# A fused set-attention and gated feed-forward kernel: centring with two-tensor instructions, GpSimd's issues ahead of its weight cast, and another written order of steps

## The chip, the cores and the metric

The kernel runs on one core of a Trainium2 chip. The core has a matrix engine (TensorE, PE in the profile, with its weight loader PEld), three engines for elementwise work (VectorE = DVE, ScalarE = ACT, GpSimd = POOL) and a queue engine (SyncE = SP). Each engine works through its own queue in order; they wait for each other by semaphores. Transfers are issued from the queues of SyncE, ScalarE or GpSimd and carried by 16 shared DMA engines. The metric is the device time of one execution, in microseconds.

## The reference

Four batches `b` of N = 12416 rows of x, each row with C = 128 numbers, meet m = 32 inducing rows.

```
def mab(q, kv):
    s = scale * (q @ kv.transpose(0, 2, 1))
    s = s - s.max(-1, keepdims=True)
    a = np.exp(s)
    a /= a.sum(-1, keepdims=True) + 1e-09
    return a @ kv
h = mab(I, x)           # [B, 32, 128]: one pass over all rows of the batch
y = mab(x, h)           # [B, N, 128]
gate = np.maximum(y @ w_gate, 0.0)      # 128 -> 1536
val = y @ w_val
out = gate * val @ w_out                # 1536 -> 128
```

All inputs and the output are float32.

## The kernel before, in words

Each output row depends on x only through its 32 attention weights over `h`. Where the sign of each gate is the same for all rows of a batch, the output is a quadratic form of these weights; the kernel works out its tables once for each batch, so that the feed-forward layer over 1536 hidden units is done on the 32 rows of `h` and not on 12416 rows of x. Checks of this run along, and a slow general kernel stands behind a branch at the end; it doesn't run here.

**Rows and tiles.** A batch is cut into six blocks `q` of 16 tiles of 128 rows (`CT = 16`, `NQ = 6`) and a remainder of one tile. `Q` counts these blocks over all batches, 0 to 23, and 24 is the four remainders together.

**The head** (`first_batch`, L264 to L450) reads batch 0 in float32 parts on SyncE's queue, casts them (L370), turns them on TensorE (L380), weighs and sums them for `h` of batch 0. The order of that is the text `HEAD`. At its end stand the weights: GpSimd casts `w_gate` to `wg` (L441), then issues the load of `w_out` to `wo` (L442) and the seven loads of batch 1 (`load_x`, L237: six of 16 tiles and the remainder, cast to float16 on the way); ScalarE casts `w_val` to `wv` (L443). Then comes `centre(0, ...)`.

**centre** (L244 to L262) makes `h` from its sums (L247, a `scalar_tensor_tensor` with two tensors), and writes it into `hT` in three copies: centred by its mean (L250), and plain twice (L254); L262 adds the mean. All are small: 128 partitions by 32 or 16 numbers. TensorE's gate matmuls (L890) need `hT`, and behind them come the tables of the batch.

**The rest** is a list of some 1,600 steps, each with its engine or engines, what it needs and which buffers it takes. What sets the order of the work on every engine is the text `ORDER`: each word of it names a step by its place in the list, the engine by a digit, and the buffers that it takes (`Plan.run`). The steps that the prediction speaks of, by the names in the code:

- `load` (GpSimd, L237): issue the load of a block; `turn` (SyncE, L763, a transposing transfer) or `tp` and `tc` (TensorE L774, then a copy L779 or L781): turn the block. `s1`, `p1`, `hz`, `ha`: weigh the block and add to the sums of `h` of its batch.
- `hw` (VectorE, L829): `zs` = the stacked identity times the weights' sums; `join` (TensorE, L839): add them over partitions; `centre` (VectorE).
- `gate`, `on`, `v`, `u`, `uj`, `tm`, `tab`, `lin`, `L`: the tables of a batch (products on VectorE or GpSimd at L980, table matmuls L999, scaling to the table `T` on ScalarE at L1011 or VectorE at L1013).
- `s2`, `p`: scores of a block and their exp (ScalarE, L514). `d`: differences of the weights (L561), two PSUM banks at once (`dd`) and two more in `mb`. `f2`: squares of two banks (ScalarE, L575). `fc`: the two single banks, squared on ScalarE (L587) or only copied on VectorE (L589); after a copy comes `fm`, a multiplication by itself (L593) on GpSimd or VectorE. `pp`, `zq`: squares (L524, L544) on either.
- `o`, `ol`: output matmuls (L619, L608); `e`: division (VectorE, L649); `st`: store (SyncE).
- `keep_busy` (L1168): filler matmuls ahead of some `d` steps.

GpSimd and VectorE steps whose kind stands in the list `shared` (L1175) are tied by hand: each GpSimd step of such a kind waits for the last VectorE step of such a kind that stands ahead of it in `ORDER` (`in_turn`, L1178). `centre` and `load` are not on that list; `hw` is.

Of the kernel before, what the change touches and what calls it, by code (L numbers as in the profile page):

```python
# [12 lines left out]
ALU = mybir.AluOpType  # L13
# [90 lines left out]
LK4LL464s4Mp4Ly4364Lz496c4LU0Ov00Le0MG000050Oz04Lo0Oy2Ow2Ox2P02O+2011O-2P1030U0M60P3012e0220600050P  # L104
21P412f10u0310710v10A10IB014B0J1PH2PE2PI2PD20CC023APb0Pc050810M10D10E1PP0PQ00Pd00304PR0PS0Pe0Pf00K1
0G1Pg1PF2PC2042PB2PG20O00429LW0810Q10P10S1053P63LX2LY03EU0PT0PJ0PK05PL00+00418LZ2PU10-1PV2PM0122PN0
Lg073PW02P53PO1101P721G00017PX0Li05Ls0040w300232Pa2Lh2Lj2Lt21K11H11I1Ck0P8011A002360x05PA11B10d000f
00g00Z041M00y2P921E21C10W014005151m0300e01621510h20M+01e020b01d00a07U0Me0Ni0Lq05H+01n1182Lr22E01y00
0341z10Y01+11330z31F31o310c22021i011j01c01P01s005431b01u11w11t11g0M8030MA03La005GE01h00o041f25M92Lb
12800202MB21k20X03MI050l00m00j00p01l4OD4NK4N940i4291MJ12A12C21922g2222001012422622310q0LQ0150r0Lc02  # L110
0k0LR10s240n22q001001732D3MR32u12r11X05A60LS04Lk0031Y0MS31213LT22s2Ld2Ph24O001Ll11O042w0012BMT04P1L
m031V02x12y2Ln2Lu0101W02+21Z21Lv14U001394Y14V11T02Q02M20001S0Lw052O04W2M31Md304Q30Mo322t3Mz332k0031
A2l12m11R01Q02N01p002P0Lx22o21q21r31U24X33W05030001072G033X1M4044R052I02R224S2311321M522722p2253MC0
123c005462K0MK0012J02L0MD13g1ML12M23e13413d1ME02MM042T012h05Mi013Mg00MF2MN2MO22i2Mj2MP022U03o00455N
V0Mh1N834NJ352z3NU32j32H03MQ22V02W02Y03Z002a03p13s13q1Pm022X233a2Pp2Pn2Po22b02Z0Pq01Pr13u000583v12c
2Pi04Ps023+03M013L03C033B03A03Y313b34T32-3Pt1Pj2Pl2Pk23i00423Pv2Pu23w13y1P-23k13j13m1Pw23O0FM03G003
I03S053703D03N0P+33P253E203T03F03R04m004213Q04q14o14n13U25k42S4Is41a4NL42Ok4O24Mq453V42d4N20413H04I
03Bs04E02700525G040N323J2Px015H1711Py1Pz1Q12Q624104a000424L0NX054D04J0MX0714c14e14b1Q02Q700Q804K04G
0NY24g00454QB1Q22QC24k14i14h143004504204F04407305QD04QE0Q334M22MY2742QH14H240035S0015749046215U25C0
45D0Mk0124705A05T1Ml15W1Q52Q424A05e000104804B25g15i15f1MV024-055205109E0MW25B050057004w01QI2NA464C4  # L120
5Y0032A4t05Z15a15c1QO353255E234z04y04x0550A+0580MZ0055604+259268041Ma15M0031BQJ026915O2QK06B05Dc05J
005443K45F4OO44N45N1QN26C25K26A32QP04QQ05P25Q16E00325Mb055+00N0016G2QT26F16I16K00346Ng35I31Nh315L37
230Mc2N126O26L15z0Mm056005-05q026M1Mn25V26W001485l0535t05p05w05u05v06a16X161216Y28m0405x256Q000138n
16R1650Mv0055o05r06406U26S2Mw16H36P38o316T3Ns305s2N40147C00104N517E27G26V37D17u051Mx026306207v1NF00
47I00109662My2NG1N6057J1NH03674OZ48M4Nt4N727M1NQ012O132OC33ON346Z36D37O004517Q17K1NI27S2Nk083Nm00Nl
27P1NR16r046y057x016s06z06t06m036x0Nn27y27H2QU276000126d027826w06h06i06u06l0NZ0007717A1Na16+207T37w
327936v26o08A005108B18C26n06p23NS00Nb049e052Ke06g08E1NT27+0030A9f1Nc26j0753Nd27F38D36k2Ne017k047m07
# [12 lines left out]
1B-02C00Cd3DA32CP3Cg2Cf1Ot03Bx01E305C10E42Ou2Bu0Ci1DQ00450C20DU1Bw0CC00Bz0By0C324DR1B+2CB0RM05DS1DE  # L140
0032ABN4AV4RN2RP2DF1CA0CD0Ch3DD3CX3Bv01RO2DI2DG1DJ3E231CE25DK00458DL1DO2E53DP3RS02C80C70RI03RQ00DM1
RT2RL2RJ2E600524E71RR2EA2RK2C60Eu041C50Cq00Co0Ev1E81C92Rg2Ra2DW00237Cm04Cu0Cr0Ct0Cw0Cp0DX1DY1Da1Cv0
F400151D002Cz0Fm030F51Cs23Re2Cx2Rb2Fn1D300C+0D40C-0Cn0Fy00349F61F81Fz1Ew30D121D50D20Dl01Do0Dm0EO005
23D62G01F+1Rd2Rc2Ri2CF4Cy4C446-4D74ES1Dj00Dw04Dg0Dh0Dx0Dy0Dn0EP1De0EQ1EI00322EK1Dp25RV3RU3EB3Dz0Ro0
Di0EJ1Dk2Rj05Dr03Rk0Df0Rn2EM1EC00105D+23ED1EG2Du0Dt0Eb05Ds0Ge022Rh2EE1E+0040BGf1Ea0Rp01EZ0F02E-1Ex0
2EH3Rq0Rr0Ey2F21Gk00426Rs0Dv2Rf2Gl1Ee00Ef0Ed0Eg0Rt2Ru2EW0FA0031AGo1Gm1EY0El02Eq04Ek0Er0FB1Eh24Ec2RW
2FC1FE1EX0Fs00057Ep0Em0Eo0Ft1R+3Fu2Es20RX03Fw1FG00100RY2RZ1FH1FI2FK2Rv04Rw0Ej0IO051Rz1G200318En2IP1
FR00R-04FS0Fp02FJ2G31G62Fq2D-4Et4BC4Dq4S00FL3Ez3S32RH2Fo22F13Fr3FO05G41Ia00122Ib1FV0FQ0FT0FU21FX0FW
0FY0G800435Ic1Ie1FZ2G91Fj00Fi0Fb01HW020FP0IQ31GA2GC2GB2HX1Gq00543Gu2Gr1Fc0Fh0Fd0Fg0GO03GD3Gv3G73Fk2
3Gs1Gw00244Fe0GN0GP0GL05Gx1G+2GG0Gy1Hu00041Ff2GK0GJ0GZ01GY0GQ0GI0Hv1G-3Hy2Fv3Gg30Hw1Hc0024AGR20Gb0H  # L150
d1IR00GW03GU0GV0Hg2GH0IS2GM2He1H00040BH42H11GT0Ga0HH05HG0HB02Gc22H53HY32H80H21GX2Ho00010Hq2Hp1HF0Gh
04GS4Fa4Fl4Gi2Gj3Hz3HC0HI0HD0L4032Hs2IU00045HA0HJ25L51Ht3Hr3HN01HL0HO0IV1HE2IY2H903IW1Hi00529Hj1Hk2
HM0HZ00HR0HS0KA040HT0Ha2HP20Hm1Im00507HQ0KB1In1IF01IE0IL02I10Io1Iq2KM00408Hb3Hl3Hh3HU2KN1KQ2ID0L703
II0IG0L82SA2IK0IJ0KO1KY00503KZ1IM21Kc2IH2I403I804I70I30I00Ka1Ig00204Ih1Ik2I90IA0I50I20IB23Ir3IT3KC3
0JG011Ii1KG0050BJH1KH1KI1I62Iy04I-02J10Iw0Ix0Iz0J703J50KK2HV4HK4Gd4Jk4KS00106IZ2S92S72KL2It05I+20J0
0J20KU1KT1KW1J32J60J80JA0JD0K-01J925Je00429Il3JI32Ji2Jf1JC0Kk00KD03K+0Kj0JB0KE2JE2Jj3KF3Jg1JM00230K
# [11 lines left out]
def square_body(ctx, tc, x, inducing, moe_w_gate, moe_w_val, moe_w_out, out):  # L168
    nc = tc.nc
    B, N, C = x.shape  # L170
    M = inducing.shape[0]
    DFF = moe_w_gate.shape[1]
    P = 128
# [70 lines left out]
    def centre(b, sums):  # L244
# [8 lines left out]
        for o, n in ((M, M), (2 * M, H)):  # L253
            nc.vector.tensor_scalar(  # L254
                out=hT[b][:, o : o + n],
                in0=h[:, 0:n],
# [7 lines left out]
    def first_batch(sp, psum):  # L264
# [179 lines left out]
        for q in range(NQ + 1):  # L444
            load_x(1, q, x16q[q] if q < NQ else x16r[1])
# [952 lines left out]
```

## Time and profile before

| | us |
|---|---|
| median of 3 runs | 240.14 |
| lowest and highest | 238.80, 240.24 |
| the profiled execution | 240.26 |
| its span, first to last instruction | 238.4 |
| granted TensorE clock, share of full | 0.994 |

The busy times of the page are sums over the span: TensorE 222.7, VectorE 205.4, ScalarE 201.7, GpSimd 128.7 us. A busy TensorE is not TensorE at its peak, since matmuls overlap and their ends are modelled. In a row of the timeline the columns are start and duration in us, engine, line, operation, written tile <- read tiles, and in brackets the engine's idle time ahead of it with what ended that. Lines are those of the kernel before.

### The profile page before, as it was taken

What the parts mean: (1) busy time and instruction counts of PE and PEld (TensorE: products, weight loads), DVE (VectorE), ACT (ScalarE), POOL (GpSimd) and SP (SyncE); (2) the same over time, 40 slices, a digit from 0 to 9 for tenths busy, and PEclk for the clock granted to TensorE, in tenths of its full rate; (3) what the DMA queues carried; (4) which work ended last, traced back from release to release, by engine and by line L of the source; (5) the groups of instructions that cost most, each with busy time, mean ns of one, the idle gap of its engine ahead of it and who ended that gap; (6) DMA issues with size and microseconds to landing.
All of it is one profiled execution on the core that took longest, in us unless ns stands there. A gap on an engine that the chain in (4) does not pass through costs nothing.

```text
span 238.4 us, 9612 instructions
## 1 busy us (share of the span) xinstructions
PE 222.7 (93%) x4092; PEld 174.3 (73%) x4092; DVE 205.4 (86%) x433; ACT 201.7 (85%) x366; POOL 128.7 (54%) x164
## 2 busy tenths in 40 slices
PE   5869888999999999999999999998999999999990
PEld 1768457787787888887788778875787777777870
DVE  4665798899589999869999999899999998989792
ACT  3665798799999889898989988898999999998940
POOL 4444905619493139795731527687143568963900
PEclk9999999999999999999999999999999999999997
DMA  6998899989998698969995999121292060665764
GB/s 212 413 396 317 99 214 204 197 160 191 197 202 219 150 272 308 245 109 236 289 269 99 265 168 411 50 116 64 91 355 88 4 267 3 268 247 206 287 228 151
DMA packets 36240, 49.25 MB, mean 207 GB/s; under 512 B 24384, under 2 KB 25056, under 8 KB 36192
## 3 DMA queue, kind: packets, MB, share of 16 engines
q1 hardware_dynamic: 31568, 38.64, 50.5%
q0 software_dynamic: 4576, 9.93, 23.7%
q8 instruction: 33, 0.54, 0.9%
q14 instruction: 15, 0.12, 0.2%
q10 hardware_dynamic: 48, 0.02, 0.1%
HBM read 27.80 MB, written 25.43 MB: 223 GB/s over the span
## 4 chain that ended last, share of the span: by engine, by line
PE 66%; DMA 16%; DVE 11%; ACT 3%; issue 2%; POOL 0%; SPq 0%; DVEq 0%; ACTq 0%
PE mb L619 34%; PE dd L561 7%; DMA x<-in_x_dram 6%; DMA x16q<-in_x_dram 6%; PE mb L561 4%; PE mb L608 4%; DVE osb L649 4%; DMA w<-in_moe_w_val_dram 4%; PE mb L804 3%; PE mb L505 3%; PE mb L790 3%; PE mb L774 2%; PE mb L999 2%; ACT F L575 2%; DVE F L589 2%
## 5 line engine op out<-in xcount | busy, mean ns | idle before, releaser
L619 PE MATMUL mb<-T,F 128*128 128x128 f16 x1536 | 107.8, 219 | 0.1
L575 ACT ACTIVATE F<-dd 128x1024 f16<-128x1024 f32 x97 | 100.1, 1032 | 9.2 <-PE dd L561 4.0
L619 PEld LDWEIGHTS <-F 128*128 128x128 f16 x1536 | 87.4, 98 | 18.1 <-issue 16.6
L593 POOL TENSOR_TENSOR F<-F 128x512 f16<-128x512 f16 x59 | 60.6, 1042 | 31.8 <-DVE pp L524 8.8
L587 ACT ACTIVATE F<-mb 128x512 f16<-128x512 f32 x120 | 69.1, 607 | 2.9 <-PE mb L561 1.6
L649 DVE TENSOR_TENSOR osb<-mb,zr 128x512 f32<-128x512 f32 x97 | 64.4, 680 | 6.2 <-PE mb L619 4.2
L589 DVE CAST F<-mb 128x512 f16<-128x512 f32 x74 | 49.6, 683 | 4.2 <-PE dd L561 2.6
L561 PE MATMUL mb<-p,diff 32*128 32x512 f16 (+1 forms) x200 | 39.8, 376 | 0.0
L561 PE MATMUL dd<-p,diff 32*128 32x512 f16 (+1 forms) x200 | 37.6, 375 | 1.4 <-ACT F L575 1.3
L524 POOL TENSOR_TENSOR pp<-p 128x512 f16<-128x512 f16 (+1 forms) x21 | 21.2, 1010 | 12.4 <-PE mb L619 5.5
L561 PEld LDWEIGHTS <-diff 32*128 32x128 f16 x400 | 13.8, 91 | 10.8 <-issue 5.2
L999 PE MATMUL mb<-wo,U 128*128 128x128 f16 x264 | 18.7, 219 | 0.0
L994 POOL TENSOR_TENSOR U<-U,U 128x1536 f16<-128x1536 f16 x3 | 9.3, 3099 | 16.7 <-DVE zr L544 7.8
L999 PEld LDWEIGHTS <-U 128*128 128x128 f16 x264 | 15.2, 97 | 1.8 <-issue 1.6
L514 ACT ACTIVATE p<-mb 128x512 f16<-128x512 f32 (+1 forms) x25 | 14.7, 593 | 2.0 <-PE mb L505 1.1
L608 PE MATMUL mb<-L,pp 32*128 32x128 f16 x384 | 16.2, 216 | 0.0
L980 DVE TENSOR_TENSOR U<-ga,va 128x1536 f16<-128x1536 f16 x15 | 14.4, 969 | 0.2
L980 DVE TENSOR_TENSOR U<-va,ga 128x1536 f16<-128x1536 f16 x15 | 14.5, 970 | 0.0
L384 DVE COPY xT<-xT_ps 128x1024 f16<-128x1024 f16 (+1 forms) x15 | 8.6, 581 | 5.9 <-PE xT_ps L380 5.9
L370 POOL CAST x16f<-x 128x512 f16<-128x512 f32 (+2 forms) x14 | 7.4, 531 | 11.4 <-DMA x<-in_x_dram 11.4
L370 ACT CAST x16f<-x 128x512 f16<-128x512 f32 (+2 forms) x15 | 7.8, 517 | 6.8 <-DMA x<-in_x_dram 6.7
L608 PEld LDWEIGHTS <-pp 32*128 32x128 f16 x384 | 10.1, 93 | 4.6 <-issue 0.5
(158 smaller groups left out, 305.2 us busy)
## 6 DMA issues: line engine op xcount, KB each, us to landing
out_dram<-osb SPq DMA_DIRECT2D x44, 512.0 KB, 4.4
x16q<-in_x_dram POOLq DMA_DIRECT2D x18, 512.0 KB, 9.4
x<-in_x_dram SPq DMA_DIRECT2D x9, 512.0 KB, 7.1
out_dram<-osb SPq DMA_DIRECT2D x9, 256.0 KB, 2.0
x<-in_x_dram SPq DMA_DIRECT2D x6, 256.0 KB, 9.2
w<-in_moe_w_gate_dram SPq DMA_DIRECT2D x1, 768.0 KB, 8.3
w<-in_moe_w_val_dram SPq DMA_DIRECT2D x1, 768.0 KB, 8.9
wo<-in_moe_w_out_dram POOLq DMA_DIRECT2D x1, 384.0 KB, 5.6
```

The source lines that it names most:

```text
L370: f(out=dst[:, a:b, :], in_=x32[:, a:b, :])
L524: engines[e].tensor_tensor(out=p2b[slot["pp", Q]][:, 0:w], in0=a, in1=a, op=ALU.mult)
L561: nc.tensor.matmul(bs[r][:, o], diff[rows, 4 * jj : 4 * jj + 4, :].rearrange("p k m -> p (k m)"), pb[slot["p", Q]][rows, 0:w], start=True, ...
L575: act.activation(out=Fb[slot["F", Q, j]][:, pair(j), :], in_=dd, func=AF.Square, accum_out=None if k is None else spread(Q, k),)
L587: act.activation(out=dst, in_=src, func=AF.Square, **more)
L589: dve.tensor_copy(out=dst, in_=src)
L593: engines[e].tensor_tensor(out=a, in0=a, in1=a, op=ALU.mult)
L608: nc.tensor.matmul(mb[slot["m", "o", Q, r]][:, t * P : (t + 1) * P], p2b[slot["pp", Q]][rows, t * P : (t + 1) * P], L[(Q // NQ) % 2][rows, :],
L619: nc.tensor.matmul(ps[:, t * P : (t + 1) * P], Fb[slot["F", Q, j]][:, r, t * P : (t + 1) * P], T[Q // NQ][:, j, :], start=start, stop=stop,)
L649: dve.tensor_tensor(out=o[:, 4 * (r % 2) : 4 * (r % 2) + 4, :], in0=mb[slot["m", "o", Q, r]].rearrange("p (t c) -> p t c", t=4), in1=rz.un ...
L980: engines[e].tensor_tensor(out=U[i][:, :, 4 * j : 4 * j + 4, :], in0=a[:, :, 0:M].unsqueeze(2).broadcast_to([P, NFF, 4, M]), in1=bass.AP(c ...
L999: nc.tensor.matmul(ps, U[i][:, t, 4 * j : 4 * j + 4, :].rearrange("p k m -> p (k m)"), wo[:, t, :], start=(i, t) == (0, 0), stop=(i, t) == ...
```

## The change

Four things change.

1. In `centre`, L250 and the two instructions of L254 become `scalar_tensor_tensor` with a second tensor in place of a second scalar: the mean spread over the columns, and a tile of ones. The same is done to `hw` (L829). The numbers that they compute stay the same.
2. At the end of the head GpSimd issues the load of `w_out` and the first load of batch 1 ahead of its cast of `w_gate`; the other loads of batch 1 come behind the cast. ScalarE's cast of `w_val` stays the first of its queue at that place.
3. `hw` is taken off the list `shared`.
4. `ORDER` is another text: the same steps, in another order in places, some of them on another engine. One `d` step has three filler matmuls ahead of it in place of four.

```
-        nc.vector.tensor_scalar(
-            out=hT[b][:, 0:M], in0=h, scalar1=float(M), scalar2=mean, op0=ALU.mult, op1=ALU.subtract
+        nc.vector.scalar_tensor_tensor(
+            out=hT[b][:, 0:M],
+            in0=h,
+            scalar=float(M),
+            in1=mean.broadcast_to([P, M]),
+            op0=ALU.mult,
+            op1=ALU.subtract,
         )
         for o, n in ((M, M), (2 * M, H)):
-            nc.vector.tensor_scalar(
+            nc.vector.scalar_tensor_tensor(
                 out=hT[b][:, o : o + n],
                 in0=h[:, 0:n],
-                scalar1=float(M),
-                scalar2=1.0,
+                scalar=float(M),
+                in1=ones32[:, 0:n],
                 op0=ALU.mult,
                 op1=ALU.mult,
             )
...
-        nc.gpsimd.tensor_copy(out=wg, in_=w32[0])
         nc.gpsimd.dma_start(out=wo, in_=moe_w_out.rearrange("(i p) c -> p i c", p=P))
-        nc.scalar.copy(out=wv, in_=w32[1])
         for q in range(NQ + 1):
             load_x(1, q, x16q[q] if q < NQ else x16r[1])
+            if q == 0:
+                nc.gpsimd.tensor_copy(out=wg, in_=w32[0])
+        nc.scalar.copy(out=wv, in_=w32[1])
...
-        dve.tensor_scalar(
+        dve.scalar_tensor_tensor(
             out=zs,
             in0=stackI[:, 0:M],
-            scalar1=hz[:, M : M + 1],
-            scalar2=1.0,
+            scalar=hz[:, M : M + 1],
+            in1=ones32[:, 0:M],
             op0=ALU.mult,
             op1=ALU.mult,
         )
...
-    shared = set("u uj lin fm pp gabs zq hw ts".split())
+    shared = set("u uj lin fm pp gabs zq ts".split())
...
 ORDER = """
-LK4LL464s4Mp4Ly4364Lz496c4LU0Ov00Le0MG000050Oz04Lo0Oy2Ow2Ox2P02O+2011O-2P1030U0M60P3012e0220600050P
...
+O24Mp4Ly4LK4NK43646c4LL462E0Oz00Ov05Le0M6000040LU0Lo0Ow2Oy2O+2Ox2P303011P02O-2P101MG0P4103020600540
...
```

More of the change, by code (lines that the diff above doesn't have):

```diff
@@ new lines @@
+21m0101A00026Lj1PA10w320z31L3053Pa2P921C21E21B10a040b00Z00Y03+00W0314005051n11510c201621D31F30f00g0
+Lq020d00e01y001441b05182M+01e01d01c01z11931P002010h21+2Lr21s003131i0NV0La0041-31o311731u11t11w21f25
+1h0MA012M803Lb1MB2M92Ni028001522C12912A20i41g01j00j040p020q0MI030k02B3MJ21k20X022005110m01l42312420
+o0LQ0130r00s24253MR3LR10l0Lc002610n22q0053AMS31LS02Lk0012r12u2LT2Ld2Ph22s1Ll14O0422w003201Y002y22+2
+4P12x1Lu015Lm01A601X02N031V01Q041x3Md302g20Mo32Ln21O0Lv14U002194W24Q324V14Y22Q01S01R01W01Z21M20051T
@@ L163, in square_kernel @@
+93L224Jc1JZ1Kw0JJ02Ko0Kr0Kp0Kq0JK2Ky2Ks2K503J-05K40Ja1LA00204S42JL3SB2LC1LD1LB1Jl014K60K70K825K10K0
+0J+0K22L34Kn4Kt4K94Kz4S52Jx0Jp0Ju0Jv0Jw0Jy20Jq0Jo0S602SC2Jz4K34S82LE00LF0Jr0LG0LH0Js2SD2Jt4LI21SE03
+SF2LJ4SG4"""
 def square_kernel(tc, x, inducing, moe_w_gate, moe_w_val, moe_w_out, out):
```

104 lines of the change are left out of this document (48 added, 56 removed).

## The prediction

> **What bounds the kernel now.** I read the page first: how full each engine is, and which chain ended last.
>
> ```profile
> span 238.4 us, 9612 instructions
> ...
> PE 222.7 (93%) x4092; PEld 174.3 (73%) x4092; DVE 205.4 (86%) x433; ACT 201.7 (85%) x366; POOL 128.7 (54%) x164
> ...
> PE 66%; DMA 16%; DVE 11%; ACT 3%; issue 2%; POOL 0%; SPq 0%; DVEq 0%; ACTq 0%
> ```
>
> TensorE, VectorE and ScalarE are all nearly full, GpSimd is half empty. The chain is TensorE's for two thirds of the span, but a sixth of it is transfers, so next I followed the chain of waits in order of time.
>
> ```profile
> 15.64 8.87 DMA w<-in_moe_w_val_dram
> ...
> 25.91 1.03 POOL x16q L237 x2
> 26.94 14.14 DMA x16q<-in_x_dram
> ```
>
> Up to 26.94 + 14.14 = 41.1 us the kernel's end hangs on transfers: the second weight matrix, then the loads of batch 1, of which the fourth is only there when TensorE is to turn it (L774). Behind that the chain is engine work. The third view is the share of the DMA engines by stage (last column but one; the busy times are PE, PEld, DVE, ACT, POOL).
>
> ```profile
> 22.00:24.00 2.00, 2.00 (x51) 1.76 (x49) 1.09 (x3) 1.22 (x5) 1.27 (x1) 1.00 0.23 86
> 24.00:26.00 2.00, 1.83 (x27) 0.97 (x24) 1.02 (x7) 1.46 (x1) 2.00 (x4) 1.00 0.00 0
> 26.00:28.00 2.00, 2.00 (x37) 1.05 (x36) 1.58 (x6) 1.43 (x5) 2.00 (x5) 1.00 1.05 104
> 30.00:36.00 6.00, 4.91 (x69) 3.50 (x68) 5.55 (x8) 6.00 (x13) 0.36 (x2) 1.00 1.05 212
> ```
>
> Between 22 and 26 us the DMA engines are used 0.23 x 2 + 0.00 x 2 = 0.5 of 4 us, so 3.5 us lie idle; behind 26 us they are full (over 1.0). The hole has its reason on GpSimd's queue:
>
> ```profile
> 20.85 0.40 POOL L370 CAST x16f<-x 128x256 f16<-128x256 f32 x1 [0.36 <-DMA x<-in_x_dram]
> 22.73 1.47 POOL L441 CAST wg<-w 128x1536 f16<-128x1536 f32 x1 [1.48 <-DMA w<-in_moe_w_gate_dram]
> 24.14 1.22 POOL L442 DMA_DIRECT2D wo<-in_moe_w_out_dram  x1
> 25.36 3.20 POOL L237 DMA_DIRECT2D x16q<-in_x_dram  x6
> ```
>
> GpSimd is done with batch 0 at 21.25 us, waits 1.48 us for the gate weights, casts them, and only then issues the output weights and the loads.
>
> **Part 1: the issues ahead of the cast.** Moved are one wo issue and one load issue (3.20 / 6 = 0.53 us); nothing of theirs waits. They would start at 21.25 instead of 24.14 us: 2.9 us earlier. The cast would start at 21.25 + 1.22 + 0.53 = 23.0 instead of 22.73 us, 0.3 us later, and end near 24.5. The other five loads and the remainder follow it, from 24.5 instead of 25.9 us: 1.4 us earlier. The first packets of wo are about 1.9 us behind their issue (issue at 24.14, engines idle until 26.0), so the stream would start near 23.1 us. Before, wo and the first load kept the engines until SyncE's queue, which waits for that load, could go on at 32.88 us (row below), so some 6.9 us of traffic are in front of the second load, whose issue at 24.5 comes long before 23.1 + 6.9 = 30.0 us. So the whole stream moves by 2.9 us, and the fourth load lands near 38.2 instead of 41.1 us.
>
> ```profile
> 32.88 14.94 SPq L763 DMA_TRANSPOSE xT<-x16q  x2
> 35.34 0.90 PEld L774 LDWEIGHTS <-x16q 128*128 128x128 f16 x16 [1.09 <-DMA x16q<-in_x_dram]
> 35.34 1.07 PE L774 MATMUL mb<-eye,x16q 128*128 128x128 f16 x16 [0.80 <-ACT F L587]
> 41.12 0.34 PE L774 MATMUL mb<-eye,x16q 128*128 128x128 f16 x3 [0.61 <-DMA x16q<-in_x_dram]
> ```
>
> What that is worth is read from who waited for it. TensorE stood idle twice, 0.80 us at 35.34 (the weight loader's row names the transfer) and 0.61 us at 41.12: 1.41 us, and its weight loader 1.09 at the first. With a lead of 2.9 us both waits go, since the second turn would then be wanted near 41.1 - 0.61 - 0.80 = 39.7 and its data are there at 38.2. What is late next is ScalarE (6.00 of 6 us in 30 to 36) and VectorE (5.55 of 6): they are why I take the 1.41 us and not the 2.9. Below, the gain is nothing if these two set the pace already; above, it is 2.9.
>
> Covers. The cast of wg, 0.3 us later, ends at 24.5; its first user:
>
> ```profile
> 25.69 0.39 PE L890 MATMUL mb<-hT,wg 128*128 128x81 f16 x6 [0.17 <-DVE hT L262]
> 26.58 0.46 PE L890 MATMUL mb<-hT,wv 128*128 128x49 f16 x12
> 24.54 1.47 ACT L443 CAST wv<-w 128x1536 f16<-128x1536 f32 x1 [0.63 <-DMA w<-in_moe_w_val_dram]
> 26.59 0.60 ACT L514 ACTIVATE p<-mb 128x512 f16<-128x512 f32 x1 [0.57 <-PE mb L505]
> ```
>
> It waits for the centring (hT), not for wg: 1.2 us of cover. Narrower is the value side. The tail of w_val lands at 24.5 us and would now share the engines with wo from 23.1 on; ScalarE's cast stands in front of its first exp and had 0.57 us of slack, so a tail late by up to 0.57 us costs nothing, and each tenth more costs a tenth. Only 0.5 us of traffic was left after 22 us, so I put it at zero, 0.5 us as the upper end. [...]
>
> **Part 2: centring and weighing with two tensors.** Four instructions change form: L250, the two of L254 (in each of four centrings) and L829 (three times). Nothing is added.
>
> ```profile
> L247 DVE SCALAR_TENSOR_TENSOR h<-hz,rzs x3: 192/236/1010, 68.0 to 159.8; 128x32 f32<-128x32 f32 x3
> L250 DVE TENSOR_SCALAR hT<-h,hb x4: 242/292/944, 25.1 to 160.0; 128x32 f16<-128x32 f32 x4
> L254 DVE TENSOR_SCALAR hT<-h x8: 166/180/1010, 25.2 to 161.0; 128x32 f16<-128x32 f32 x4, 128x16 f16<-128x16 f32 x4
> L829 DVE TENSOR_SCALAR zs<-stackI,hz x3: 232/241/243, 66.7 to 153.9; 128x32 f32<-128x32 f32 x3
> ```
>
> L247 has the new form already and the same size: 192 ns at its shortest, against 242, 166 and 232. So the forms cost the same within 0.05 us each: nothing. What matters are the maxima near 1 us. Each lies under a GpSimd multiplication and ends with it:
>
> ```profile
> 113.09 2.04 POOL L593 TENSOR_TENSOR F<-F 128x512 f16<-128x512 f16 x2 [0.90 <-DVE zs L829]
> 114.17 1.01 DVE L247 SCALAR_TENSOR_TENSOR h<-hz,rzs 128x32 f32<-128x32 f32 x1
> 115.74 0.32 PE L890 MATMUL mb<-hT,wv 128*128 128x49 f16 x6 [0.21 <-DVE hT L262]
> 159.91 2.06 POOL L593 TENSOR_TENSOR F<-F 128x512 f16<-128x512 f16 x2
> 160.04 0.94 DVE L250 TENSOR_SCALAR hT<-h,hb 128x32 f16<-128x32 f32 x1
> 160.90 1.09 DVE L254 TENSOR_SCALAR hT<-h 128x32 f16<-128x32 f32 x2
> 162.11 0.40 PE L890 MATMUL mb<-hT,wg 128*128 128x81 f16 x6 [0.73 <-DVE hT L262]
> ```
>
> In the centring of batch 3 the scalar form L250 took 0.94 us and ended at 160.98, where the first of two multiplications ends (half of 159.91 to 161.97 is 160.94); the pair of L254 ended at 161.99 with the second. In batch 2 it was L247, a two-tensor instruction, that took 1.01 us and ended at 115.18 with the multiplications (115.13). So both forms wait for GpSimd, and the swap saves nothing: I take 0. TensorE lost 0.21 and 0.73 us to these, so 0.94 us is the most that this part can bring. [...]
>
> **Part 3: "hw" leaves the list.** Steps on that list make a later GpSimd product wait for the last listed VectorE step. The POOL row at 113.09 shows it: 0.90 us of waiting for zs (L829). Without it GpSimd would have begun 0.9 us earlier and been in the middle of a product when L829 came, and L829, now with two SBUF inputs, would have waited as L247 did: up to 1.01 - 0.19 = 0.82 us. Behind L829 stands the join on TensorE, which takes its turn in order, so a late L829 stalls everything behind it there. From both sides: nothing if no product is running, 3 x 0.82 = 2.5 us if all three meet a full one. In the new order the three hw steps stand behind one, two and three products that VectorE has time to outlast in part, so I take 0.3 us: one of the three meets a product, and waits a third of the 0.82.
>
> **Part 4: the order.** Read step by step, the new text holds the same steps with some moved between engines: VectorE gets one more bank cast (75 for 74), four more table scalings (14 for 10) and three fewer multiplications (12 for 15); GpSimd four more of these (63 for 59); the rest are single moves both ways. One filler matmul of seven goes.
>
> ```profile
> L589 DVE CAST F<-mb 128x512 f16<-128x512 f32 x74 | 49.6, 683 | 4.2 <-PE dd L561 2.6 <-PE mb L561 0.9
> L593 DVE TENSOR_TENSOR F<-F 128x512 f16<-128x512 f16 x15 | 6.3, 438 | 0.0
> L1013 DVE TENSOR_SCALAR T<-mb,half 128x128 f16<-128x128 f32 x10 | 3.4, 337 | 0.4
> 160.00:180.00 20.00, 18.92 (x304) 14.14 (x302) 19.83 (x37) 18.77 (x32) 10.05 (x12) 1.00 0.43 170
> ```
>
> That is 0.68 + 4 x 0.34 - 3 x 0.44 = 0.7 us more on VectorE, which in the stage of the tables of batch 3 has none to spare (19.83 of 20 us) while TensorE idles 1.08 there. The order could give up to that 1.08 back, or lose the 0.7. I take 0: the profile of before can't rank two orders.
>
> **The sum**, against the profiled execution of 240.26 us (the span of 238.4 and 1.9 around it; 0.12 above the median of the three runs, 240.14): 240.26 - 1.41 (transfers) + 0 (casts, forms, order) + 0.3 (hw) = 239.15, say 239.1 us.
>
> **Rivals.** (a) The lead of the loads carries on whole, because the new order uses it: 240.26 - 2.9 = 237.4 us. For it speaks that the chain is DMA without a break to 41.1; against it, that ScalarE and VectorE are full from 30 to 36 us. (b) The other side, slower: GpSimd, no longer held, runs its products into both the weighing and the centring. Price: 2.5 us for three L829, and the centring of each batch as in batch 3 (0.94 - 0.24 for L250 and 1.01 - 0.17 for one L254, 1.5 us) in place of 1.5 and 0.82 in two: 3 x 1.5 - 2.3 = 2.2; all on the path 4.7, less the 1.4 of the loads: 243.6 us. It decides from 1.4 us of collisions on. [...] (c) The transfers are hidden anyway: a load that lands earlier only exposes ScalarE, and the time stays at 240.3 us. For it, 6.00 of 6 us; against, the two waits on TensorE. (d) The two-tensor forms escape GpSimd after all: 239.1 - 0.3 - 0.94 = 237.9; the 1.01 us of L247 speaks against.
>
> **How the numbers follow.** Chances: forecast 0.40, (a) 0.20, (b) 0.18, (c) 0.17, (d) 0.05. About 1% (2.4 us) is what a measurement of this kernel can tell from no change: faster is below 237.7, slower above 242.5. Faster: most of (a), half of (d) and a little of the forecast with an order that helps, 0.24. Slower: (b) nearly whole, and little else, 0.17. Within: 0.59. The range: the forecast's own goes from 239.1 - 1.08 to 239.1 + 0.7 + 0.5 (order, w_val); to leave out 2 in 10 it takes in (a) with some help from the order, 236.6, and the nearer half of (b), 242.4.
>
> **What would show it.** Right: wo issued near 21.3 us, DMA share in 24 to 26 us about 1, no wait for x16q in front of L774. Part 2: an L250 or L254 near 1 us still, under an L593 of GpSimd. Part 3: an L829 over 0.3 us and an idle TensorE in front of L839. Wrong: TensorE's waits of 35 and 41 us back under another name (c), ScalarE's cast of wv ending after 26.6 us, or a difference that arises behind 60 us and hangs on the order alone.

## The result and the profile after

| | median us | executions | ratio to before, 95% interval |
|---|---|---|---|
| before | 240.3 (238.8 to 241.76) | 20 | |
| after | 242.46 (240.77 to 244.89) | 20 | 1.0083 [1.006, 1.0106] |

The changed kernel is slower, by 0.83% or 2.0 us, where 239.1 us, less than before, were forecast; its median lies at the upper end of the range (242.4). The ratio leaves out two executions in a slower state of the chip (244.44 and 244.89 us); the median of the other 18 is 242.34 us. The profiled execution took 242.89 us. Three lines of its page, the span, the busy times and the shares of the chain of waits:

```profile
span 241.1 us, 9594 instructions
...
PE 224.1 (93%) x4091; PEld 175.9 (73%) x4091; DVE 207.4 (86%) x437; ACT 201.8 (84%) x362; POOL 130.8 (54%) x165
...
PE 71%; DMA 9%; ACT 7%; DVE 5%; issue 3%; POOL 3%; SPq 0%; DVEq 0%; ACTq 0%; POOLq 0%
```

Transfers fell from 16% of the chain to 9%. TensorE, VectorE and GpSimd have 1.4 to 2.1 us more on their account, ScalarE 0.1, and GpSimd has 3% of the chain for 0%. (The lines behind the head are now some six higher: the weighing L829 is L835, the join L839 is L845, L254 is L259, the squares L575 and L587 are L581 and L593, the cast L589 is L595, the multiplication L593 is L599, the division L649 is L655, the turn L774 is L780.)

**The loads.** The timeline of the kernel after, and behind it the same stretches by windows (columns as before):

```profile
20.64 1.22 POOL L446 DMA_DIRECT2D wo<-in_moe_w_out_dram  x1
21.85 0.55 POOL L237 DMA_DIRECT2D x16q<-in_x_dram  x1
22.39 1.48 POOL L450 CAST wg<-w 128x1536 f16<-128x1536 f32 x1
23.80 2.65 POOL L237 DMA_DIRECT2D x16q<-in_x_dram  x5
24.58 1.47 ACT L451 CAST wv<-w 128x1536 f16<-128x1536 f32 x1 [1.24 <-DMA w<-in_moe_w_val_dram]
...
31.41 14.67 SPq L769 DMA_TRANSPOSE xT<-x16q  x2
...
34.38 1.06 PE L780 MATMUL mb<-eye,x16q 128*128 128x128 f16 x16
```

```profile
22.00:24.00 2.00, 2.00 (x48) 1.65 (x46) 0.91 (x4) 0.83 (x3) 2.00 (x3) 1.00 0.72 106
24.00:26.00 2.00, 1.85 (x21) 0.85 (x19) 0.92 (x9) 1.42 (x1) 2.00 (x5) 1.00 1.61 183
```

The output weights are issued 3.5 us earlier (20.64 for 24.14), the DMA engines' hole from 22 to 26 us is filled (0.72 and 1.61 for 0.23 and 0.00), the first load is there 1.5 us earlier (SyncE's queue goes on at 31.41 for 32.88), and no wait for x16q stands in front of TensorE's turns any more. In this execution the whole head ran 0.6 us earlier than in the one of before (the last step of the first centring starts at 24.8 us, before at 25.4), so 0.6 us of each lead don't come from the change. ScalarE's cast of w_val begins at 24.58 for 24.54, which against the earlier head is 0.6 us late: it waited 1.24 us for the transfer, where before it waited 0.63. TensorE's weight loader waited 0.30 us for it here, its matmuls didn't.

**The weighing of batch 2.** Timeline of the kernel after; "PE L845" is the join:

```profile
111.38 0.54 POOL L237 DMA_DIRECT2D x16r<-in_x_dram  x1
...
111.61 2.42 DVE L835 SCALAR_TENSOR_TENSOR zs<-stackI,hz,ones 128x32 f32<-128x32 f32 x1
...
111.93 2.05 POOL L599 TENSOR_TENSOR F<-F 128x512 f16<-128x512 f16 x2
...
113.96 1.28 DVE L655 TENSOR_TENSOR osb<-mb,zr 128x512 f32<-128x512 f32 x2
114.69 0.41 PE L845 MATMUL mb<-zs,ones 128*128 128x32 f32 x2 [1.88 <-DVE osb L655]
...
116.20 0.60 ACT L593 ACTIVATE F<-mb 128x512 f16<-128x512 f32 x1 [2.12 <-PE mb L567]
...
116.93 2.04 POOL L599 TENSOR_TENSOR F<-F 128x512 f16<-128x512 f16 x2 [2.96 <-DVE F L595]
```

GpSimd, which no longer waits for zs, starts two multiplications at 111.93, and zs, which took 0.24 us before, now takes 2.42 us: it ends (114.03) not with the first product, but with the second (113.98). Both products stand behind this `hw` in `ORDER` (they are `fm 9.2.0` and `fm 8.1.0`), so they are those that the list had made wait. Two divisions (osb, L655) stand behind it on VectorE, and the first of them must free the PSUM bank that the join writes to. So TensorE stands idle for 1.88 us, then ScalarE for 2.12 and GpSimd for 2.96. The window from 100 to 120 us, first of before, then of after:

```profile
100.00:120.00 20.00, 19.63 (x416) 15.88 (x413) 17.46 (x43) 18.76 (x36) 14.04 (x19) 1.00 0.93 209
```

```profile
100.00:120.00 20.00, 18.02 (x342) 14.43 (x340) 16.79 (x38) 15.34 (x28) 14.10 (x18) 0.91 1.05 232
```

TensorE lost 1.6 us of busy time, and the granted clock fell to 0.91 on average: it was 0.5 from 115.43 to 118.84, 0.7 us behind the end of the idle time.

**The centring.** Groups of the kernel after (minimum, median and maximum in ns; first and last start):

```profile
L259 DVE SCALAR_TENSOR_TENSOR hT<-h,ones x8: 161/180/1029, 24.6 to 163.5; 128x32 f16<-128x32 f32 x4, 128x16 f16<-128x16 f32 x4
L250 DVE SCALAR_TENSOR_TENSOR hT<-h,hb x4: 191/191/906, 24.5 to 162.6; 128x32 f16<-128x32 f32 x4
L247 DVE SCALAR_TENSOR_TENSOR h<-hz,rzs x3: 192/193/193, 66.6 to 162.4; 128x32 f32<-128x32 f32 x3
```

The two-tensor forms cost no more than the old ones when they run free (at their shortest 0.191 us for 0.242 in L250, 0.161 for 0.166 in L259, before L254), and still meet GpSimd (0.906 and 1.029 us).

### The profile page after: what moved, and what is told of

It reads as the page before. It is cut to its first block, busy times and chain, and to the rows that moved or that the text cites. A ratio compares the mean times of both kernels' runs of the same rounds, so it can differ in the third digit from the quotient of the medians.

```text
span 241.1 us, 9594 instructions
## 1 busy us (share of the span) xinstructions
PE 224.1 (93%) x4091; PEld 175.9 (73%) x4091; DVE 207.4 (86%) x437; ACT 201.8 (84%) x362; POOL 130.8 (54%) x165
## 4 chain that ended last, share of the span: by engine, by line
PE 71%; DMA 9%; ACT 7%; DVE 5%; issue 3%; POOL 3%; SPq 0%; DVEq 0%; ACTq 0%; POOLq 0%
PE mb L625 35%; PE dd L567 7%; DMA x<-in_x_dram 6%; PE mb L567 5%; PE mb L614 4%; PE mb L1005 4%; ACT F L593 3%; ACT F L581 3%; DMA x16q<-in_x_dram 3%; PE mb L511 2%; PE mb L796 2%; PE mb L780 2%; PE mb L810 2%; DVE osb L655 2%; PE mb L896 1%
## 5 line engine op out<-in xcount | busy, mean ns | idle before, releaser
L581 ACT ACTIVATE F<-dd 128x1024 f16<-128x1024 f32 x97 | 100.1, 1032 | 9.1 <-PE mb L567 4.0
L599 POOL TENSOR_TENSOR F<-F 128x512 f16<-128x512 f16 x63 | 64.8, 1040 | 25.3 <-DVE F L595 12.7
L593 ACT ACTIVATE F<-mb 128x512 f16<-128x512 f32 x119 | 69.8, 608 | 4.5 <-PE mb L567 3.6
L655 DVE TENSOR_TENSOR osb<-mb,zr 128x512 f32<-128x512 f32 x97 | 63.9, 682 | 6.1 <-PE mb L625 3.8
L595 DVE CAST F<-mb 128x512 f16<-128x512 f32 x75 | 50.1, 680 | 5.7 <-PE mb L567 4.2
L530 POOL TENSOR_TENSOR pp<-p 128x512 f16<-128x512 f16 (+1 forms) x20 | 20.0, 1008 | 17.9 <-PE mb L625 7.4
L614 PE MATMUL mb<-L,pp 32*128 32x128 f16 x384 | 16.7, 218 | 0.2 <-DVE osb L655 0.2
L550 POOL TENSOR_TENSOR zr<-zr 128x16 f32<-128x16 f32 (+1 forms) x22 | 4.6, 219 | 16.5 <-DVE U L986 7.8
```

The costliest lines, as they stand in the source:

```text
L530: engines[e].tensor_tensor(out=p2b[slot["pp", Q]][:, 0:w], in0=a, in1=a, op=ALU.mult)
L581: act.activation(out=Fb[slot["F", Q, j]][:, pair(j), :], in_=dd, func=AF.Square, accum_out=None if k is None else spread(Q, k),)
L593: act.activation(out=dst, in_=src, func=AF.Square, **more)
L595: dve.tensor_copy(out=dst, in_=src)
L599: engines[e].tensor_tensor(out=a, in0=a, in1=a, op=ALU.mult)
L614: nc.tensor.matmul(mb[slot["m", "o", Q, r]][:, t * P : (t + 1) * P], p2b[slot["pp", Q]][rows, t * P : (t + 1) * P], L[(Q // NQ) % 2][rows, :],
```

## The experiments

Each edit below is on the kernel after, or on the one before where it says so. For where the time goes I use marks that every trace has: the last step of each of the four centrings (L262 before, L267 after). The table has the times between them, in us, and from the last of them to the end of the span.

| kernel | ratio to before | 0 to 1 | 1 to 2 | 2 to 3 | 3 to end |
|---|---|---|---|---|---|
| before | 1 | 43.15 | 47.00 | 46.37 | 76.5 |
| e3: before, new head | 0.9926 [0.99, 0.9953] | 41.83 | 46.96 | 46.39 | 76.5 |
| e5: e3 with the new forms | 0.9955 [0.9929, 0.998] | 41.48 | 46.67 | 46.53 | 76.5 |
| e1: after, hw listed (e5 with the new order) | 1.0044 [1.0026, 1.0063] | 43.04 | 46.64 | 47.45 | 77.3 |
| after | 1.0083 [1.006, 1.0106] | 43.20 | 48.06 | 47.56 | 77.5 |
| e6: e1, step "other" early | 1.0018 [0.9999, 1.0038] | 43.24 | 46.49 | 47.95 | 76.4 |
| e11: e6, step Lr later | 0.9946 [0.9923, 0.9968] | 44.04 | 46.17 | 45.86 | 76.3 |

The first five rows take the change apart, one part at a time: head, forms, order, list. The last two move single steps of the new order. Each stretch of time is from one execution, and the ratios are from several: e1 and e6 have the same order between the first and the last centring, and differ by 0.5 us from the third to the fourth. (Some expectations count from the first step of a centring, L247, so their figures differ a little.)

### The head: e3 and e4

e3 is the kernel before with the new order of issues alone:

```
-        nc.gpsimd.tensor_copy(out=wg, in_=w32[0])
         nc.gpsimd.dma_start(out=wo, in_=...)
...
             load_x(1, q, x16q[q] if q < NQ else x16r[1])
+            if q == 0:
+                nc.gpsimd.tensor_copy(out=wg, in_=w32[0])
```

> The kernel before with the new order of issues and casts at the head's end, nothing else. The prediction's step: loads 2.9 us earlier, TensorE's two waits of 1.41 us go, 238.9 us, ratio 0.994. Rival (ScalarE and VectorE set the pace): 0.3 us or less, 0.999 to 1.001. Theory 3 (the earlier transfers delay the value weights): slower, over 1.002, and the cast of wv ends after 26.6 us.

Measured: 238.0 us (before beside it 239.78). By the table 1.3 us are gone, all of them before the second centring (41.83 for 43.15). The turns of batch 1 on TensorE in e3, with no wait for x16q ahead of any:

```profile
33.32 1.07 PE L775 MATMUL mb<-eye,x16q 128*128 128x128 f16 x16
...
36.33 0.61 PE L775 MATMUL mb<-eye,x16q 128*128 128x128 f16 x8
...
37.88 1.06 PE L775 MATMUL mb<-eye,x16q 128*128 128x128 f16 x16
```

e4 is the reverse, the kernel after with the old head (the same lines back).

> The changed kernel with the old order of issues and casts at the head's end. If the head brings 1.4 us, this run is slower than the changed kernel by 1 to 2.9 us, 243.5 to 245 us, ratio 1.013 to 1.02; if ScalarE and VectorE hide it, 242 to 242.7 us. If the meeting of zs with the products hangs on small shifts (theory 1), zs of batch 2 may be free here and the time below 242 us in spite of the later loads.

Measured: 244.42 us, ratio 1.0191 [1.0157, 1.0225]; from the first to the second centring 44.72 us for 43.20. So in this kernel the head is worth 1.5 us on the traces and, by the ratios (1.0191 - 1.0083), 2.6 us of the medians. It helps in either kernel.

It isn't free of risk. The tail of w_val now comes in a stretch where the DMA engines are used (0.72 and 1.61 from 22 to 26 us in the kernel after, 0.23 and 0.00 before), and ScalarE's wait for it is longer, by an amount that differs between executions: 0.63 us before and 0.66 in e4, with the old head, 1.24 in the kernel after and 1.50 in e3. In the trace of e11 (below), which has the same head, ScalarE waited 2.07 us for it and TensorE 0.78 us for the cast (in that of e7 0.29 us):

```profile
25.08 1.47 ACT L451 CAST wv<-w 128x1536 f16<-128x1536 f32 x1 [2.07 <-DMA w<-in_moe_w_val_dram]
...
26.60 0.47 PE L896 MATMUL mb<-hT,wv 128*128 128x49 f16 x12 [0.78 <-ACT wv L451]
```

### The forms: e5

e5 is e3 with L250, L254 and L829 in the two-tensor form, and hw still on the list.

> The kernel before with the new head (as in the third run, ratio 0.9926 to before) and the two-tensor forms in the centring and the weighing; hw stays on the list, the order is the old one. If the forms cost nothing, as predicted: 238.0 us, ratio 0.990 to 0.995, and the centrings of batches 2 and 3 still hold an instruction near 1 us. Rival (the forms are part of the loss): 0.3 to 1 us more, 0.995 to 0.998. Rival (d) (the two-tensor forms escape GpSimd): no centring instruction over 0.3 us, 237 us.

Measured: 239.06 us. Its interval overlaps that of e3, and its trace is 0.5 us shorter from the first centring on, so no cost of the forms can be told from these runs. Do they escape GpSimd?

```profile
L259 DVE SCALAR_TENSOR_TENSOR hT<-h,ones x8: 160/180/1072, 25.2 to 159.9; 128x32 f16<-128x32 f32 x4, 128x16 f16<-128x16 f32 x4
L250 DVE SCALAR_TENSOR_TENSOR hT<-h,hb x4: 191/206/956, 25.1 to 158.0; 128x32 f16<-128x32 f32 x4
L247 DVE SCALAR_TENSOR_TENSOR h<-hz,rzs x3: 191/242/1020, 66.3 to 157.7; 128x32 f32<-128x32 f32 x3
```

No: the maxima are as large as those of before (0.944 for L250, 1.010 for L254 and L247).

### The list: e1, e2, e9, e10, e8

e1 puts hw back on it in the kernel after:

```
-    shared = set("u uj lin fm pp gabs zq ts".split())
+    shared = set("u uj lin fm pp gabs zq hw ts".split())
```

> The changed kernel with hw put back on the list, nothing else. Theory 1 (the weighing of batch 2, no longer protected, waits 2.2 us for two GpSimd products, TensorE idles 1.9 us behind it and then gets half its clock for 3.4 us): the three zs instructions take 0.16 to 0.26 us, no stretch of half clock near 115 us, and the time falls by 2 to 3.5 us, to 239 to 240.5 us, ratio to the kernel before 0.995 to 1.000. Theory 2 (the new order is slower by itself): the time stays at 242 to 242.5 us, 1.007 to 1.010.

Measured: 240.98 us, between what the two theories said. Rows of e1:

```profile
111.60 0.25 DVE L835 SCALAR_TENSOR_TENSOR zs<-stackI,hz,ones 128x32 f32<-128x32 f32 x1
111.93 2.04 POOL L599 TENSOR_TENSOR F<-F 128x512 f16<-128x512 f16 x2
...
112.63 0.36 PE L845 MATMUL mb<-zs,ones 128*128 128x32 f32 x2
```

All three zs take 0.25 us or less, TensorE doesn't wait for the join, no stretch of half clock follows (the granted clock is 1.00 from 100 to 120 us), and from the second to the third centring there are 46.64 us for 48.06. GpSimd's products start at 111.93 in both kernels: being held for zs cost GpSimd nothing that can be seen here. So the list is worth 1.4 us on the trace and 0.9 us by the ratios, whose intervals just touch. Yet the time stays above before: the list is not the whole loss.

e2 takes hw off the list in the kernel before, and changes nothing else.

> The kernel before with hw taken off the list, nothing else. Theory 1: in the trace of before GpSimd waited 0.90 us for zs of batch 2; without that wait its product is running when zs comes, so zs of batch 2 takes 0.6 to 2 us and the time rises by 0.5 to 3 us, ratio 1.002 to 1.012. Theory 2: nothing happens but that GpSimd is 0.9 us earlier; 240.3 us, 0.998 to 1.002.

Measured: 240.33 us beside 239.78, ratio 1.0017 [0.9996, 1.0038]: nothing that can be told from no change. Its timeline at the weighing of batch 1:

```profile
66.06 1.30 DVE L829 TENSOR_SCALAR zs<-stackI,hz 128x32 f32<-128x32 f32 x1
66.25 1.06 POOL L593 TENSOR_TENSOR F<-F 128x512 f16<-128x512 f16 x1
...
67.42 0.41 PE L839 MATMUL mb<-zs,ones 128*128 128x32 f32 x2 [0.65 <-DVE zs L829]
```

The old form waits for the product as well (1.30 us, to the end of the product at 67.31), and TensorE for it (0.65). The zs of batch 2, of which the expectation spoke, took only 0.46 us. From the first to the second centring there are 44.93 us for 43.15, but from the second to the third 45.35 for 47.00: what the wait had cost was made up. In the old order one zs met one whole product; in the new order one met two.

e9 asks whether the form has a part in that: the kernel after, hw unlisted, zs in its old form.

```
-        dve.scalar_tensor_tensor(
+        dve.tensor_scalar(
             out=zs,
             in0=stackI[:, 0:M],
-            scalar=hz[:, M : M + 1],
-            in1=ones32[:, 0:M],
+            scalar1=hz[:, M : M + 1],
+            scalar2=1.0,
```

> The kernel after, with hw unlisted as there, but zs written in its old form, with one SBUF tensor and a scalar in place of two tensors. Theory (the list decides, the form doesn't matter: e2 showed the old form waiting 1.30 us in batch 1): zs of batch 2 takes over 1 us again, and if it meets both products 2.4 us, with the idle of about 1.9 us in front of the join and the half clock behind it: 242.0 to 243.0 us, ratio near 1.008. Rival (the form decides: the one with two SBUF inputs loses both turns, the old one loses none or one): zs takes 0.25 to 1.3 us, no half clock, 240.7 to 241.6 us, ratio near 1.004 as with hw listed.

Measured: 242.41 us, ratio 1.0093 [1.0058, 1.0129]. Group and timeline of e9:

```profile
L835 DVE TENSOR_SCALAR zs<-stackI,hz x3: 145/241/2409, 65.7 to 157.3; 128x32 f32<-128x32 f32 x3
```

```profile
115.00 0.41 PE L845 MATMUL mb<-zs,ones 128*128 128x32 f32 x2 [1.63 <-DVE osb L655]
```

2.41 us, with one SBUF tensor as with two. The list decides, the form doesn't.

e10 takes the meeting away in another way: hw stays off the list, and ScalarE computes zs.

```
-        dve.scalar_tensor_tensor(out=zs, ...)
+        act.activation(out=zs, in_=stackI[:, 0:M], func=AF.Copy, scale=hz[:, M : M + 1])
```

> The kernel after, hw unlisted, with zs computed on ScalarE (a copy scaled by hz) in place of VectorE, so that GpSimd is not held for it and it can't meet a GpSimd product on VectorE. Theory (the loss of the unlisted hw is the meeting and what it stalls): zs takes under 0.5 us in every batch, no idle over 1 us in front of the join of batch 2, no half clock, the interval from the second to the third centring 47.0 us or less as with hw listed (47.12; the kernel after 48.91): 240.3 to 241.3 us. Rival (ScalarE is full, and a zs in its queue stands behind an exp or a square): the join waits for it up to 0.6 us in each batch and the time stays at 242 us or above.

Measured: 241.31 us, ratio 1.0041 [1.0008, 1.0074], as e1. zs takes 0.31 to 0.36 us on ScalarE, and the join of batch 2 comes with no wait:

```profile
113.32 0.36 PE L838 MATMUL mb<-zs,ones 128*128 128x32 f32 x2
```

So the loss is the meeting itself, and either way out of it is worth the same.

e8 was to price the half clock: nine filler matmuls ahead of the join of batch 2 in the kernel after, so that TensorE isn't idle there.

```
+        if b == 2:
+            keep_busy(slot["m", "h", b], 9)
         nc.tensor.matmul(mb[slot["m", "h", b]][:, 0:M], ones32, zs, ...)
```

> The changed kernel with nine filler matmuls (9 x 0.21 = 1.9 us) in TensorE's queue ahead of the join of batch 2, where it idles 1.88 us. If the idling is what halves TensorE's clock for 3.4 us from 115.4 us on: no half clock there, and the time falls by 0.5 to 1.7 us, ratio 1.001 to 1.006 against 1.0083. Rival (the clock has another cause, or half the clock costs nothing because the other engines set the pace): the same time, 1.007 to 1.010.

Measured: 243.35 us, ratio 1.013 [1.0095, 1.0165]; the experiment missed its aim.

```profile
115.28 2.10 PE L1178 MATMUL mb<-diff,eye 128*128 128x512 f16 x9 [1.88 <-DVE osb L655]
117.22 0.30 PE L847 MATMUL mb<-zs,ones 128*128 128x32 f32 x2
```

The fillers write to the join's own bank, so they waited for the same division and then ran ahead of the join, 1.9 us of pure delay. No half stretch followed in the profiled execution (granted clock 1.00 from 100 to 120 us), but that says little, since it isn't in every execution: in the profiled one of e9 much the same stall, 1.63 us, stands without it (1.00 as well). A stretch of 3.4 us at half clock takes 0.007 off the mean clock of an execution (3.41 x 0.5 / 241), so I counted those with a mean under 0.99. With the stall (after, e4, e9) there are 19 of 34, in the same order without the stall (e1, e6, e7, e10, e11) 2 of 58. So, by the mean clocks, behind the stall such a stretch comes in about half of the executions. It isn't bound to this place: of the executions of the kernel before that ran beside the experiments 13 of 96 are under 0.99 too, and the mean doesn't tell where.

What it costs is known only roughly. By the medians of the executions under 0.99 and of the others it is 0.9 us in the kernel after (242.69 and 241.76, 9 each) and 0.4 in e9. On the traces there are 95.62 us from the second to the fourth centring in the kernel after, and 93.91 in e9, where the stall stands alone. What the stall costs without the stretch stays open: by the medians, each against the kernel before beside it, 0.3 us (241.76 / 240.3 = 1.0061, e1 240.98 / 239.78 = 1.0050); by the traces nothing, since e9 makes it up by the fourth centring (e1 94.09).

### The order: e6, e7, e11, e12

e5 and e1 differ in the order alone: 0.9955 to 1.0044, 2.1 us (1.4 to 2.9 by the intervals). It is the largest loss of the change. On the traces it is 3.3 us: 1.6 between the first two centrings, 0.9 between the last two, 0.9 behind them. TensorE's busy time in the same stretches says that it stood idle for 2.1 us of these (1.0, 0.6 and 0.4, and 0.1 between the second and the third centring). In the rest it counts as busy, and no run says what made it slower.

**Behind the last centring.** In the new order VectorE makes the check step "other" (L1113, L1114) in the last 17 of its steps, in the old one 28 from the end. e6 is e1 with that step moved ahead (VectorE's queue):

```
+ other, most 0, e 21.0, e 21.1, ...
...
- e 23.0, fc 22.1.1, other, e 23.3, zr 22, ...
+ e 23.0, fc 22.1.1, e 23.3, zr 22, ...
```

> The first run (changed kernel, hw on the list, 1.0044) with one step of the order moved: the check called other (three VectorE instructions, 1.8 us with a wait for GpSimd in the second) stands ahead of the division of block 21, where VectorE waits 0.9 us for TensorE, and not in the last 12 us. If the new order loses 1.1 us in its tail through this step: 0.8 to 1.2 us less, ratio 0.999 to 1.001, and the time from the centring of batch 3 to the end falls from 79.9 to 78.9 us. Rival (the tail is TensorE's own, from the order of the last matmuls): unchanged, 1.003 to 1.006.

Measured: 240.55 us, ratio 1.0018 [0.9999, 1.0038] (e1 1.0044; the intervals overlap, and 0.999 to 1.001 was expected), and from the last centring to the end 76.4 us for 77.3, the expected 1.0. Rows of the kernel after, then of e6:

```profile
225.83 1.10 DVE L1113 SCALAR_TENSOR_TENSOR chk<-rzs,chk 128x128 f32<-128x128 f32 x1
226.85 0.67 DVE L1114 TENSOR_REDUCE tsum<-Lr 128x1 f32<-128x512 f16 x1
...
228.18 0.61 PE L625 MATMUL mb<-T,F 128*128 128x128 f16 x8 [0.50 <-DVE osb L655]
```

```profile
217.86 0.29 DVE L1113 SCALAR_TENSOR_TENSOR chk<-rzs,chk 128x128 f32<-128x128 f32 x1
```

**Between the first two.** There one copy of the centring of batch 1 takes over 1 us under a GpSimd square (L250 1.08 us in e1, L259 1.03 in the kernel after). e7 is e1 with centre on the list as well, so that GpSimd waits for it.

```
+    shared = set("u uj lin fm pp gabs zq hw ts centre".split())
```

> The first run with the step centre put on the list too, so that GpSimd's square of block 4, which stands behind the centring of batch 1 in the order, waits for it. In the first run that square starts 0.2 us into the centring, one copy waits 1.0 us for it, and TensorE idles 0.79 us. If the meeting costs what TensorE idled: 0.6 to 0.8 us less, ratio 1.001 to 1.002, and the centring of batch 1 takes 0.55 us in place of 1.4. Rival (other work fills in): no change, 1.004.

Measured: 241.3 us, ratio 1.006 [1.0036, 1.0083], no better than e1. The first interval fell as it should, by 0.88 us (43.04 to 42.16), and the next one grew by 0.71 (46.64 to 47.35). GpSimd now stands still for VectorE there, which is a likely reason, but not a tested one:

```profile
113.90 2.03 POOL L599 TENSOR_TENSOR F<-F 128x512 f16<-128x512 f16 x2 [3.06 <-DVE hT L267]
```

The rest of the 1.6 us there was not tried.

**Between the last two.** The timeline of e6 (the kernel after and e1 have the same waits, 1.0 to 1.1 us):

```profile
131.63 0.95 DVE L1000 TENSOR_TENSOR U<-U,U 128x1536 f16<-128x1536 f16 x1
132.50 0.28 DVE L497 TENSOR_SCALAR L<-mb 128x128 f16<-128x128 f32 x1
...
132.81 0.27 ACT L978 ACTIVATE Lr<-mb 32x128 f16<-32x128 f32 x1 [0.99 <-DVE L L497]
...
134.76 0.39 PE L567 MATMUL dd<-p,diff 32*128 32x512 f16 x2 [1.01 <-ACT F L581]
```

The new order puts a table product (uj, L1000, 0.95 us) on VectorE ahead of L. On ScalarE the little Lr waits for L, and behind Lr stand the squares that free TensorE's banks. In the old order (here e5) this wait was 0.48 us, and TensorE's 0.36:

```profile
129.44 0.27 ACT L978 ACTIVATE Lr<-mb 32x128 f16<-32x128 f32 x1 [0.48 <-DVE L L497]
...
131.87 0.39 PE L567 MATMUL dd<-p,diff 32*128 32x512 f16 x2 [0.36 <-ACT F L581]
```

Nobody needs Lr before the check "other" and the block of the remainders, both near the end. e11 is e6 with Lr of batch 2 two steps later on ScalarE:

```
- ..., fc 11.3.0, Lr 2, fc 11.3.1, f2 11.3, p 15, ...
+ ..., fc 11.3.0, fc 11.3.1, f2 11.3, Lr 2, p 15, ...
```

> The new order with hw listed and the last step early (as e6), and one more step moved: Lr of batch 2 on ScalarE, which there waits 0.99 us for VectorE's L and holds up the squares behind it (TensorE then waits 1.01 us; in the old order 0.36), stands two steps later, behind the copy and the square. Theory (the new order's loss comes from such single places, and this is the largest one between the third and the fourth centring): ScalarE's wait in front of L978 goes, TensorE's wait near 134.8 us falls from 1.01 to 0.4 us or less, the interval from the third to the fourth centring falls from 46.4 by 0.6 us to 45.8 or less, and the median from 240.55 to about 240.0 (ratio near 1.000). Rival (VectorE is the bound of that stretch, and TensorE then waits for a bank cast in place of the square): the interval and the median stay within 0.2 us.

Measured: 238.69 us, ratio 0.9946 [0.9923, 0.9968], from 1.0018: three times the expected 0.6 us. The windows from 124 to 136 us, first e6, then e11:

```profile
124.00:136.00 12.00, 10.51 (x179) 8.39 (x176) 11.17 (x20) 9.70 (x17) 3.47 (x5) 1.00 1.07 259
```

```profile
124.00:136.00 12.00, 12.00 (x227) 9.96 (x224) 11.67 (x22) 11.85 (x23) 4.09 (x4) 1.00 1.11 252
...
132.09 0.27 ACT L978 ACTIVATE Lr<-mb 32x128 f16<-32x128 f32 x1
```

TensorE is busy 12.00 of 12 us for 10.51, ScalarE 11.85 for 9.70. Of the 1.49 us that TensorE was idle in e6, 1.01 are the wait for the squares; 0.47 us lie at 127.71 us, ahead of Lr, and aren't in e1. So the interval is better compared with that of e1, whose order is the same there: 45.86 us for 47.45, 1.6 us less. That is still more than the wait of 1.0 us. It may be that ScalarE and TensorE, which wait for each other in turn there (squares free banks, differences fill them), passed one late step on to the next ones, but no run shows that. (The 44.04 us of e11 between the first two centrings hold a stretch of half clock, 27.61 to 31.02 us, behind the wait for w_val shown above; the mean granted clock is 0.91 from 22 to 40 us.) With the two steps moved, the new order is level with the old one (e11 0.9946, e5 0.9955), though not place by place: on the traces it stays longer between the first two centrings, and it is 0.5 and 0.7 us shorter than e5 between the next ones, so e11 does more there than undo a loss.

e12 makes the same move in the old order (there it is three steps, to behind the same square), on e3, the kernel with the lowest ratio of this study.

> The kernel before with the new head (as e3, 238.0 us, ratio 0.9926) and Lr of batch 2 moved in the same way in the old order, where TensorE waits 0.36 us at that place. Theory (this wait is on the path): the interval from the third to the fourth centring falls from 45.59 us by up to 0.36, and the median is 237.6 to 238.0, ratio 0.991 to 0.993. Rival (VectorE bounds the stretch): no change, 238.0 us.

Measured: 238.96 us, ratio 0.9975 [0.9957, 0.9992], worse than e3. Neither theory had that.

```profile
130.88 0.27 ACT L973 ACTIVATE Lr<-mb 32x128 f16<-32x128 f32 x1
...
131.20 1.05 PE L620 MATMUL mb<-T,F 128*128 128x128 f16 x16 [1.39 <-ACT Lr L973]
```

Lr reads a PSUM bank, and in the old order an output block takes that bank next: with Lr later, TensorE waits 1.39 us for it. From the third to the fourth centring there are 47.38 us for 46.39. The same move gains 1.6 us on that stretch in one order and loses 1.0 in the other; by the ratios it gains 1.7 and loses 1.2.

## Why the prediction was wrong

- **Part 1, the issues ahead of the cast: right in its main step.** 1.41 us were forecast, the two waits of TensorE; e3 shows both gone, 1.3 us less on the trace, and 1.8 (0.74%, with an interval from 0.5% to 1.0%) of the medians. The lead of 2.9 us for the whole stream was less exact: counted from the first centring, the fourth load lands 2.5 us earlier in e3 and 1.4 us in the kernel after. Of the covers that of the gate weights held. That of w_val, put at zero with 0.5 us as the upper end, held in e3 and in the kernel after, but not in each execution (0.78 us of TensorE in e11). Rivals (a) and (c) fall: with the head alone, the gain is neither the whole lead nor nothing.
- **Part 2, the forms: right.** No cost that can be told, and each form meets GpSimd as before (up to 0.906 and 1.029 us in the kernel after for 0.944 and 1.010); rival (d) falls.
- **Part 3, hw off the list: the kind of loss was right, the size was wrong.** Forecast 0.3 us, one zs that waits a third of 0.82; measured 0.9 us of the medians and 1.4 on the trace from the second to the third centring (after against e1). The term counted the products that stand ahead of the hw steps in the new order; the two that zs met stand behind it, and only the list had kept them behind. It also assumed that a zs meets one product and is through when that ends. It waited for two in a row (2.42 us), which no row of before had shown. What stood behind it on VectorE, two divisions, one of which frees the join's bank, was not looked at, nor that a stretch of half clock can follow (3.41 us at 0.5). A bound of 2.5 us stood in the text, as three meetings of one product each; it came in about that size as one meeting of two, which is luck.
- **Part 4, the order: this is the step that failed.** "I take 0: the profile of before can't rank two orders", with 0.7 us as the most that it could lose, from VectorE's busy time. It cost 2.1 us, about what the head gained or more. The bound was a sum of durations on one engine; what the runs showed in its place are waits at single places: a check step moved into the last 12 us (0.6 us by the ratios of e1 and e6, whose intervals overlap; 1.0 on the traces), and a wait of ScalarE that stood ahead of the squares (moving it gained 1.7 us by the ratios of e6 and e11). With hindsight both can be read from the two texts of the order: which steps come to stand in front of L, and behind which steps nothing is left to hide in. The loss between the first two centrings was the largest on the traces, and its cause stays open.
- **Rival (b), slower at 243.6 us,** had the sign and half of the mechanism. But the centring did not become worse (two steps near 1 us, three before), and of the three zs only one met a product.

In sum, from the ratios: head -1.8, forms +0.7 (within error), order +2.1, list +0.9, together +2.0 us. The four add up because each is the step from one ratio to the next; each is uncertain by 0.6 to 0.9 us.

Still open: why zs of batch 2 waited for both products. It began 0.32 us ahead of the first (111.61 for 111.93), while GpSimd was still issuing a transfer (111.38 to 111.92), and the same picture stands in e4 (113.07 for 113.39) and, with one product, in batch 1 of e2 (66.06 for 66.25). In e1 and e6, where the product follows the issue just as closely but had to wait for zs, zs takes 0.25 us. And the rest of the loss between the first two centrings.

## What to carry to other kernels

Before an order by hand is taken, look in each in-order queue for small steps that wait for another engine (a copy, a check) and at what stands right behind them; here moving one such step gained 1.7 us, where its own wait had been 1.0. A later place is better only if the step holds no bank that somebody needs (in e12 TensorE waited 1.39 us for one). And before a guard between two engines is taken away (here zs, 0.24 us when free, took 2.42 beside two GpSimd products), count not one meeting, but as many operations as the other engine has ready behind the guard, and what is queued behind the loser; and see whether the guard costs anything at all.

## What the runs showed of the hardware

- A 128x32 VectorE instruction (0.24 us when free) that met two GpSimd products in a row waited for both: 2.42 us (after, e4, e8) with two SBUF tensors, 2.41 (e9) with one. By the recorded starts VectorE was first by 0.32 us (after: 111.61 for 111.93), and yet it ended (114.03) with the second product (113.98). No run here shows why.
- The issue of a DMA on GpSimd didn't hold zs: in e1 and e6 it ran within the issue of the remainder's load (e1: 111.60 to 111.85 in 111.36 to 111.90) and took 0.25 us.
- In the kernel after, 1.88 us of idle TensorE were followed by 3.41 us at a granted clock of 0.5 (115.43 to 118.84). In the 3.41 us ahead of that stretch (112.02 to 115.43) TensorE was busy for 1.53 us, and for 3.42 of the 3.42 us before. In the trace of e9 much the same stall (1.63 us) was followed by none (1.00 from 100 to 120 us); by the mean clocks the stretch comes in about half of the executions with the stall (19 of 34). In e11 a stretch of the same length (27.61 to 31.02 us) came behind a wait of TensorE of 0.78 us. No run here shows what decides when it comes.
